# Segment sums on the vector engine, scan products held behind the next block's first product, and memory V products two steps sooner

## The chip, the cores and the metric

The kernel runs on one core of one Trainium2 chip. The metric is device time in microseconds (us) of one execution. The engines are named as the profile names them: PE is TensorE (PEld its weight loads), DVE is VectorE, ACT is ScalarE, POOL is GpSimd, SP is SyncE.

## The reference, cut to what matters

Two independent halves are computed and put side by side into a (1, 2048, 2048) bf16 result.

```python
# half A: a diagonal complex state space over 2048 steps, 1024 states
Bu = einsum('bld,pd->blp', x, B_bar)
for t in range(L):
    h = Lam_bar * h + Bu[:, t]
y = 2 * einsum('blp,dp->bld', hs, C).real + x * Dskip

# half B: 64 segments of 32 rows, 32 heads of 128, 8 memory rows carried from segment to segment
for s in range(64):
    h = concat([mem, x[s * 32:(s + 1) * 32]])      # 40 rows
    q, k, v = h @ Wq, h @ Wk, h @ Wv
    o = softmax(mask(q k^T / sqrt(128))) @ v @ Wo
    mem = o[:8]; out[s] = o[8:]
```

In half A the kernel rotates the complex recurrence into real scans: a block of 512 steps and 128 states is multiplied by a table of cosines and sines, scanned with a real decay, and multiplied back. In half B it does not run 64 segments one after the other: it takes a guess at the memory rows from the mean of each segment, works on all segments at once, and checks the guess at the end. The segment means of x are the "segment sums" of the title. The check and the fallback behind it are the same in all kernels here.

## The kernel before: what the change and the argument touch

There are 32 scan blocks (8 groups of states `pc`, 4 stretches of time `tb`). TensorE's instructions are pinned in program order. Each scan block is followed by four tiles of V products (`v_x`), so TensorE does 16 products into psU, then 32 into psP, and so on, for some 310 us. The other engines' order is chosen by a scheduler that follows the program, except where it says `keep_in_program_order`.

```python
def stage1(self, pc, tb):                          # one scan block
    t3, r3 = self.tabs
    u = k.ps("U", (128, 2, TB))                    # psU: two buffers
    for i in range(2):
        for c in range(KC):
            PE.matmul(u[:, i, :], self.bt[:, i, c, :], self.xT[:, c, ...], ...)          # 16 products
    pr = self.wp.tile([128, 2, 2, TB], FP32, name="a_pr", bufs=2)
    V.tensor_tensor(pr[:], u[:]..., view(t3, ...), ALU.mult)        # the first product: it frees psU
    w = pr[:, :, 0, :]
    V.tensor_tensor(w, w, pr[:, :, 1, :], ALU.add)
    g = self.wp.tile([128, 2, TB], BF16, name="a_g", bufs=2)
    for j in range(2):
        V.tensor_tensor_scan(w[:, j, :], rb, w[:, j, :], ...)
        S.activation(g[:, j, :], w[:, j, :], ACT.Copy)              # a_g, on ScalarE
    # ... carry into the next block, on GpSimd ...
    n = self.wp.tile([128, 2, 2, TB], BF16, name="a_n", bufs=1)
    h = self.wp.tile([128, 2, TB], BF16, name="a_h", bufs=2)
    V.tensor_tensor(n[:], g[:]..., view(r3, ...), ALU.mult)         # waits for a_g
    V.tensor_tensor(h[:], n[:, :, 0, :], n[:, :, 1, :], ALU.add)
    k.SP.dma_start(self.hs[tb][:, pc, :, :], h[:])

def v_x(self, hb, q, w):                           # four tiles of V
    st = self.next_st()                            # staging tile: two buffers
    for i in range(4):
        p = k.ps("P")[:]                           # psP: three buffers
        self.v_mm(p, w, 4 * q + i)                 # 8 products
        k.copy("s", st[:, i, :, 0:E], p...)        # the eviction psP -> b_vst, on ScalarE
    k.nc.scalar.dma_start(vx[...], st[...])        # the staging store b_vst -> b_vx, from ScalarE's queue

def sum_x(self, tmp):                              # segment sums of x, on TensorE
    # loads tile t of x (128 rows, row-major) as xr, four tiles ahead
    p = k.ps("R")
    for t in range(TT):                            # 16 tiles, one yield each
        for c in range(KC):
            k.PE.matmul(p[:, o:o + 4], xr[:, c * 128:(c + 1) * 128], k.ind[:], ...)      # 8 products of 4 columns
        yield
    # ... scaled into xbar ...

# main loop, for scan block n:
if n == 1: next(sx)
if n >= 3:
    for _ in range(2): next(sx, None)
a.stage1(pc, q)
if q == 2 and pc + 1 < PC:
    a.tables(pc + 1)                               # cosines, sines: VectorE and ScalarE

# second stage, step i of 32:
if i in (26, 28): vm = b.v_mem((i - 26) // 2, wv[(i - 26) // 2])     # V of the memory rows, heads 0-3 and 4-7
if 26 <= i < 30: next(vm)
```

## Time and profile before

| | before |
|---|---|
| median of 3 runs (lowest to highest) | 1243.47 us (1243.41 to 1243.81) |
| span of the profiled run, granted clock | 1241.5 us, 1.00 |
| scan stage, first psU product to first product of the second stage | 36.41 to 348.17 us |
| TensorE waits inside the scan stage | none |

The page's table of engines (busy time, share of the span, number of instructions), and the engine line of its chain of waits, which goes back from the last instruction to whatever released each step:

```profile
PE 1230.8 (99%) x8246; PEld 658.8 (53%) x8318; DVE 667.8 (54%) x1254; ACT 266.6 (21%) x695; POOL 278.1 (22%) x442
...
PE 96%; DMA 3%; issue 0%; SPq 0%; DVE 0%
```

TensorE is busy for all but about 11 us, and it is nearly the whole chain. So only two things can shorten the run: fewer TensorE instructions, or fewer TensorE waits. The waits of TensorE in the kernel before (who waits, for whom, us in total, times, longest):

```profile
PE psR L68 <- DVE hpb L109: 1.3, 1, 1.3
PE psO L68 <- DMA b_v<-b_vx: 0.9, 1, 0.9
PE psP L68 <- DMA b_wv<-in_B_Wv_dram: 0.4, 1, 0.4
PE psU L68 <- DMA b_xr<-in_B_x_dram: 0.3, 1, 0.3
```

Three of them belong to the start. The psO wait is the first attention product, which waits for V to be read back from memory; the timeline of TensorE shows it (start, us, instruction, tile, shapes, count, and in brackets the idle time just before with its releaser):

```profile
492.37 0.34 PE L68 MATMUL psS<-b_q,b_k 128*128 128x99 bf16 x4
493.59 0.50 PE L68 MATMUL psO<-b_v,b_m 128*128 128x129 bf16 x6 [0.88 <-DMA b_v<-b_vx]
```

TensorE's timeline in the scan stage shows one period: a psU block, the V tiles, then the segment sums' products, then the next block.

```profile
57.13 3.62 PE L68 MATMUL psU<-a_xT,a_bt 128*128 128x512 bf16 x16
60.58 7.07 PE L68 MATMUL psP<-b_wv,b_xe 128*128 128x512 bf16 x31
67.49 0.54 PE L68 MATMUL psR<-ind,b_xr 128*128 128x4 bf16 x16
67.89 3.61 PE L68 MATMUL psU<-a_xT,a_bt 128*128 128x512 bf16 x16
```

The block starts are 67.89 - 57.13 = 10.76 us apart. The 48 products of a block without sums take 48 x 215.8 ns = 10.36 us, so the sixteen small products cost 0.40 us of TensorE each time, eight times: 3.2 us. (The record counts 31 products where there are 32; single matmul records can be missing, and their ends are modelled, so starts are compared here, not ends.)

VectorE's groups between 30 and 345 us (line, engine, instruction, tiles, shapes, count; busy us, mean ns of one; idle us just before them with what ended it), and two reductions from the end of the program that serve as a price list:

```profile
L275 DVE TENSOR_TENSOR a_pr<-psU,a_tabf 128x2048 f32<-128x2048 f32 x32 | 73.0, 2282 | 16.2 <-PE psU L68 14.5 <-remote 1.6
...
L294 DVE TENSOR_TENSOR a_n<-a_g,a_tabh 128x2048 bf16<-128x2048 bf16 x32 | 39.1, 1223 | 16.8 <-ACT a_g L284 16.7
```
```profile
L887 DVE TENSOR_REDUCE c_ok<-c_a 128x1 f32<-128x704 f32 x1 | 0.9, 875 | 0.0
L887 DVE TENSOR_REDUCE c_ok<-c_a 128x1 f32<-128x208 f32 x1 | 0.4, 361 | 0.0
```

VectorE waits 16.7 us for `a_g`, the ScalarE copy that stands between its own scan and its own next product. That is the wait which the hold is meant to remove. How full each engine is, in stretches of 30 us (stretch, its length, busy us and count of PE, PEld, DVE, ACT, POOL, then the granted clock, the DMA share and GB/s):

```profile
60.00:90.00 30.00, 29.79 (x179) 14.21 (x182) 24.61 (x22) 13.60 (x24) 4.68 (x9) 1.00 0.72 196
90.00:120.00 30.00, 29.84 (x180) 14.24 (x182) 25.05 (x21) 11.73 (x21) 6.21 (x12) 1.00 0.50 140
120.00:150.00 30.00, 29.84 (x166) 14.06 (x168) 26.89 (x28) 11.31 (x20) 9.97 (x15) 1.00 0.54 162
```

VectorE is the second engine here, at 25 to 27 of 30 us. Anything moved onto it in this stretch takes it close to full.

### The profile page before, as it was taken

How to read it: one execution, taken by the hardware profiler on the slowest of the kernel's cores; microseconds unless marked ns; L12 is line 12 of the kernel's file. 1: busy time of each engine (PE TensorE's matmuls, PEld its weight loads, DVE VectorE, ACT ScalarE, POOL GpSimd, SP SyncE). 2: the span in 40 equal slices, each digit the busy share in tenths (PEclk: the TensorE clock that was granted, in tenths of full speed). 3: DMA queues.
4: the chain of work that ended last, by engine and by line, in shares of the span. 5: the costliest groups of instructions: out<-in, count | busy, mean ns of one | idle time of the engine just before them, and what ended most of it. 6: DMA issues, size and time to landing. Idle time of an engine off the chain costs nothing.

```text
span 1241.5 us, 20294 instructions
## 1 busy us (share of the span) xinstructions
PE 1230.8 (99%) x8246; PEld 658.8 (53%) x8318; DVE 667.8 (54%) x1254; ACT 266.6 (21%) x695; POOL 278.1 (22%) x442
## 2 busy tenths in 40 slices
PE   9999999999999999999999999999999999999998
PEld 4444444444455555556565656556565654445444
DVE  4688899998811124666666666666666641001000
ACT  5344344443310000111112121212111210000000
POOL 4111331222322330232223232222322220000000
PEclk9999999999999999999999999999999999999999
DMA  9965444644898834675464554545564279507000
GB/s 251 267 184 158 131 120 133 156 143 118 221 325 247 267 109 106 150 200 139 109 153 108 126 135 114 131 94 140 112 146 101 59 198 252 113 17 154 17 17 27
DMA packets 322357, 178.42 MB, mean 144 GB/s; under 512 B 144666, under 2 KB 307660, under 8 KB 322260
## 3 DMA queue, kind: packets, MB, share of 16 engines
q1 hardware_dynamic: 300164, 149.53, 49.4%
q10 hardware_dynamic: 21072, 24.38, 6.0%
q0 software_dynamic: 1024, 3.17, 0.7%
q8 instruction: 66, 1.08, 0.4%
q14 instruction: 31, 0.25, 0.1%
HBM read 89.14 MB, written 53.96 MB: 115 GB/s over the span
## 4 chain that ended last, share of the span: by engine, by line
PE 96%; DMA 3%; issue 0%; SPq 0%; DVE 0%
PE psP L68 80%; PE psU L68 9%; PE psS L68 3%; PE psO L68 2%; DMA b_v<-b_vx 2%; PE psR L68 2%; DMA b_wv<-in_B_Wv_dram 1%; SPq L68 0%; DVE b_ost L95 0%; DVE b_vm L572 0%
## 5 line engine op out<-in xcount | busy, mean ns | idle before, releaser
L68 PE MATMUL psP<-b_xe,b_wq 128*128 128x480 bf16 (+1 forms) x1280 | 247.5, 343 | 0.1
L68 PE MATMUL psP<-b_xe,b_wk 128*128 128x480 bf16 (+1 forms) x1280 | 247.5, 343 | 0.0
L68 PE MATMUL psP<-b_wv,b_xe 128*128 128x512 bf16 (+2 forms) x1033 | 223.5, 372 | 1.2 <-DMA b_wv<-in_B_Wv_dram 0.4
L694 POOL TENSOR_TENSOR b_m<-b_e,maskB 99x396 bf16<-99x396 bf16 (+1 forms) x160 | 134.4, 840 | 337.0 <-ACT b_e L693 337.0
L693 ACT ACTIVATE b_e<-psS 99x396 bf16<-99x396 f32 (+3 forms) x208 | 91.3, 441 | 531.7 <-PE psS L68 523.4
L68 PEld LDWEIGHTS <-b_wk 128*128 128x128 bf16 x1280 | 119.2, 98 | 94.2
L68 PEld LDWEIGHTS <-b_xe 128*128 128x128 bf16 x1056 | 101.8, 98 | 119.6 <-issue 0.7
L68 PEld LDWEIGHTS <-b_wq 128*128 128x128 bf16 x1280 | 118.5, 98 | 87.7
L95 DVE CAST b_k<-psP 128x480 bf16<-128x480 f32 (+1 forms) x192 | 97.3, 528 | 100.9 <-PE psP L68 100.9
L95 DVE CAST b_q<-psP 128x480 bf16<-128x480 f32 (+1 forms) x192 | 97.3, 528 | 92.2 <-PE psP L68 90.9
L68 PEld LDWEIGHTS <-b_ol 128*128 128x128 bf16 x864 | 84.3, 98 | 94.4
L68 PE MATMUL psU<-a_xT,a_bt 128*128 128x512 bf16 x493 | 113.9, 379 | 1.1
L68 PE MATMUL psP<-t,a_hl 128*128 128x512 bf16 x496 | 112.1, 379 | 0.8
L95 DVE CAST b_ost<-psP 128x512 bf16<-128x512 f32 (+1 forms) x17 | 11.5, 676 | 177.6 <-PE psP L68 176.6
L68 PE MATMUL psP<-wo,b_ol 128*128 128x512 bf16 (+1 forms) x440 | 91.9, 364 | 0.4
L68 PE MATMUL psP<-t,b_ol 128*128 128x512 bf16 x408 | 91.7, 379 | 0.4
L288 POOL TENSOR_SCALAR a_tt<-a_pr,a_tabf 128x1 f32<-128x1 f32 x48 | 34.0, 709 | 242.6 <-DVE a_pr L283 242.6
L93 ACT ACTIVATE b_vst<-psP 128x512 bf16<-128x512 f32 x126 | 72.0, 588 | 72.4 <-PE psP L68 65.1
L711 DVE TENSOR_TENSOR b_ob<-psO,b_accR 99x384 bf16<-99x384 f32 x160 | 86.0, 554 | 2.2
L275 DVE TENSOR_TENSOR a_pr<-psU,a_tabf 128x2048 f32<-128x2048 f32 x32 | 73.0, 2282 | 16.2 <-PE psU L68 14.5
L68 PEld LDWEIGHTS <-a_bt 128*128 128x128 bf16 x512 | 49.2, 98 | 57.6
L68 PEld LDWEIGHTS <-a_hl 128*128 128x128 bf16 x512 | 49.0, 98 | 56.7
(204 smaller groups left out, 969.7 us busy)
## 6 DMA issues: line engine op xcount, KB each, us to landing
b_v<-b_vx SPq DMA_DIRECT2D x16, 1122.0 KB
b_wv<-in_B_Wv_dram SPq DMA_DIRECT2D x16, 1024.0 KB
b_vx<-b_vst ACTq DMA_DIRECT2D x24, 544.0 KB
b_on<-b_ob SPq DMA_DIRECT2D x15, 720.0 KB
a_hs<-a_h SPq DMA_DIRECT2D x32, 256.0 KB
b_wog<-in_B_Wo_dram SPq DMA_DIRECT2D x4, 2048.0 KB
b_wq<-in_B_Wq_dram SPq DMA_DIRECT2D x16, 512.0 KB
b_wk<-in_B_Wk_dram SPq DMA_DIRECT2D x16, 512.0 KB
```

Of the source, the lines that this page charges most:

```text
L68: r = f(*a, **kw)
L93: self.S.activation(out, in_, ACT.Copy)
L95: self.V.tensor_copy(out, in_)
L275: V.tensor_tensor(pr[:], u[:].unsqueeze(1).to_broadcast([128, 2, 2, TB]), view(t3, [[TB + 1, 2], [TB + 1, 2], [1, TB]]), ALU.mult)
L288: G.tensor_scalar(tt[:, j:j + 1], w[:, j, TB - 1:TB], t3[:, 1, TB:TB + 1], None, ALU.mult)
L693: k.S.activation(e[:, a:b, :, 0:n], s[0:GW, a:b, :, 0:n], ACT.Exp, scale=float(E) ** -0.5, accum_out=self.accE[0:GW, j:j + 1])
L694: k.G.tensor_tensor(mv[:, a:b, :, 0:n], e[:, a:b, :, 0:n], mask[0:GW, :, 0:n].unsqueeze(2).to_broadcast([GW, b - a, 2, n]), ALU.mult)
L711: V.tensor_tensor(self.ob[:, b0:b0 + n, :], o[0:GW, 0:n, 0:E], r.unsqueeze(2).to_broadcast([GW, n, E]), ALU.mult)
```

## The change

The intent is to take the small products off TensorE and give the sums to VectorE, which has x already in the transposed tile `b_xe`; to make room there by holding the last two products of a scan block (`a_n`, `a_h`) until the first product of the next block is done, so that VectorE no longer waits for `a_g` and frees psU sooner; and to start the memory V products two steps sooner, so that V lands before the first attention product. The diff, with cuts marked:

```diff
 # consts: the tile ind and its five GpSimd fills are removed          (cut)

 def stage1(self, pc, tb):
+        self.form, last = None, self.form
         ...
         V.tensor_tensor(pr[:], u[:]..., ALU.mult)
+        if last is not None:
+            last()
         w = pr[:, :, 0, :]
         ...
-        n = ...; h = ...
-        V.tensor_tensor(n[:], g[:]..., ALU.mult)
-        V.tensor_tensor(h[:], n[:, :, 0, :], n[:, :, 1, :], ALU.add)
-        k.SP.dma_start(self.hs[tb][:, pc, :, :], h[:])
+        def form():
+            n = ...; h = ...
+            k.tc.keep_in_program_order(V.tensor_tensor(n[:], g[:]..., ALU.mult))
+            V.tensor_tensor(h[:], n[:, :, 0, :], n[:, :, 1, :], ALU.add)
+            k.SP.dma_start(self.hs[tb][:, pc, :, :], h[:])
+        self.form = form

 def sum_x(self, tmp):
-        # loads of x row-major, and 8 products psR<-ind,b_xr for each of 16 tiles       (cut)
+        xs = tmp.tile([128, KC, NSEG], FP32, name="b_xr", bufs=4)
+        for j in range(TT):
+            r = V.tensor_reduce(xs[:, :, 4 * j:4 * j + 4],
+                    self.xe[:, :, 128 * j:128 * j + 128].rearrange("p c (s t) -> p c s t", s=4), AX.X, ALU.add)
+            k.tc.keep_in_program_order(r)
             yield
         # ... scaled into xbar                                                           (cut)

 # v_mem, heads 8 and up: one transposing load instead of four
-            for h in range(4):
-                k.SP.dma_start_transpose(s[:, h, 0:E], self.vmt[hb][:, h * 128:(h + 1) * 128])
+            k.SP.dma_start_transpose(s[:, :, 0:E], self.vmt[hb][:])

 # main loop
-                if n == 1:
-                    next(sx)
-                if n >= 3:
-                    for _ in range(2):
-                        next(sx, None)
                 a.stage1(pc, q)
+                for _ in range(2):
+                    next(sx, None)
 ...
+            a.form()                       # behind the last block

 # second stage
-                if i in (26, 28):
-                    vm = b.v_mem((i - 26) // 2, wv[(i - 26) // 2])
-                if 26 <= i < 30:
+                if i in (24, 26):
+                    vm = b.v_mem((i - 24) // 2, wv[(i - 24) // 2])
+                if 24 <= i < 28:
                     next(vm)
```

More of the change, by code (lines that the diff above doesn't have):

```diff
@@ L110, in consts @@
     k.S.activation(k.hpe[:], k.hpb[:], ACT.Exp)
-    k.ind = c.tile([128, 4], BF16, name="ind")
-    G.memset(k.ind[:], 0.0)
-    for j in range(4):
-        G.memset(k.ind[32 * j:32 * j + 32, j:j + 1], 1.0)
 def masks(k):
@@ L167, in __init__ @@
         self.Cre, self.Cim, self.logdt, self.Dskip, self.out = Cre, Cim, logdt, Dskip, out
+        self.form = None
         self.hs = [k.drp.tile([128, PC, 2, TB], BF16, name=f"a_hs{i}") for i in range(NB)]
@@ L291, in stage1 @@
             self.carry = nx
-        n = self.wp.tile([128, 2, 2, TB], BF16, name="a_n", bufs=1)
-        h = self.wp.tile([128, 2, TB], BF16, name="a_h", bufs=2)
-        V.tensor_tensor(n[:], g[:].unsqueeze(1).to_broadcast([128, 2, 2, TB]), view(r3, [[TB, 2], [TB, 2], [1, TB]]), ALU.mult)
-        V.tensor_tensor(h[:], n[:, :, 0, :], n[:, :, 1, :], ALU.add)
-        k.SP.dma_start(self.hs[tb][:, pc, :, :], h[:])
+        def form():
+            n = self.wp.tile([128, 2, 2, TB], BF16, name="a_n", bufs=1)
+            h = self.wp.tile([128, 2, TB], BF16, name="a_h", bufs=2)
+            k.tc.keep_in_program_order(
+                V.tensor_tensor(n[:], g[:].unsqueeze(1).to_broadcast([128, 2, 2, TB]), view(r3, [[TB, 2], [TB, 2], [1, TB]]), ALU.mult))
+            V.tensor_tensor(h[:], n[:, :, 0, :], n[:, :, 1, :], ALU.add)
+            k.SP.dma_start(self.hs[tb][:, pc, :, :], h[:])
+        self.form = form
     def s2_tiles(self, hpool, pool):
@@ L424, in sum_x @@
     def sum_x(self, tmp):
-        k = self.k
-        xrs = {}
-        def load(t):
-            if t < TT:
-                xrs[t] = tmp.tile([128, D], BF16, name="b_xr", bufs=4)
-                k.SP.dma_start(xrs[t][:], self.x[0][t * 128:(t + 1) * 128, :])
-        for t in range(4):
-            load(t)
-        yield
-        p = k.ps("R")
-        for t in range(TT):
-            xr = xrs.pop(t)
-            for c in range(KC):
-                o = c * NSEG + 4 * t
-                k.PE.matmul(p[:, o:o + 4], xr[:, c * 128:(c + 1) * 128], k.ind[:], start=True, stop=True)
-            load(t + 4)
+        k = self.k; V = k.V
+        xs = tmp.tile([128, KC, NSEG], FP32, name="b_xr", bufs=4)
+        for j in range(TT):
+            r = V.tensor_reduce(xs[:, :, 4 * j:4 * j + 4], self.xe[:, :, 128 * j:128 * j + 128].rearrange("p c (s t) -> p c s t", s=4),
+                                AX.X, ALU.add)
+            k.tc.keep_in_program_order(r)
             yield
-        pv = p[:].rearrange("p (c s) -> p c s", c=KC)
+        e = NSEG - 4
         ms = tmp.tile([128, KC], FP32, name="b_ms", bufs=1)
-        k.V.tensor_reduce(ms[:], self.m0T[:], AX.X, ALU.add)
-        k.V.tensor_scalar(self.xbar[:], pv, 1.0 / L, None, ALU.mult)
-        k.V.tensor_tensor(ms[:], ms[:], pv[:, :, 0], ALU.add)
-        k.V.tensor_scalar(self.xbar[:, :, 0], ms[:], 1.0 / L, None, ALU.mult)
+        V.tensor_reduce(ms[:], self.m0T[:], AX.X, ALU.add)
+        V.tensor_tensor(xs[:, :, e], xs[:, :, e], ms[:], ALU.add)
+        V.tensor_scalar(self.xbar[:, :, 2:NSEG - 2], xs[:, :, 0:e], 1.0 / L, None, ALU.mult)
+        V.tensor_scalar(self.xbar[:, :, 0:2], xs[:, :, e:e + 2], 1.0 / L, None, ALU.mult)
+        V.tensor_scalar(self.xbar[:, :, NSEG - 2:NSEG], xs[:, :, e + 2:NSEG], 1.0 / L, None, ALU.mult)
         yield
```

## The prediction

It was written before the changed kernel ran.

> **Bound.** TensorE: the engine table has PE busy 1230.8 of 1241.5 us, and the chain of waits is 96% PE. The stretch table gives 29.84 of every 30 us in most of the scan stage (30 to 330 us) and 500.0 of 500 us in attention. PE idles about 10 us: start, tail, and one wait between: 0.88 us at 493.6 us, where the first attention product waits for the first V tile (25.9 us from issue to landing in the chain). Only TensorE work or waits that go away move the time.
>
> **What changes.**
> 1. 128 four-column products (psR<-ind,b_xr) go. Scan blocks come 10.36 us apart without them, 10.76 us with sixteen, eight times: -3.2 us, all critical. Some 4 MB of loads go too; PE did not wait for them. The rest of PE's order is the same, but for the memory V products, which stand 6.9 us earlier.
> 2. So the V loads start about 6.9 us sooner: -0.9 us. One transposing load for four costs PE nothing.
> 3. VectorE gets 16 reductions of 1024 elements, two behind each of the first eight blocks. The trace has reductions of 208 and 704 elements at 361 and 875 ns: about 1.2 us each by estimate, 19 us. The Trainium skill ("VectorE: DVE Perf Modes", perf-mode tier table) gives a reduce only the 1x mode, in bf16 too; 205 ns for 64 bf16 elements agree.
> 4. a_n and a_h go behind the next block's first product. VectorE's wait of 0.70 us for a_g goes (24 times, 16.7 us in the table of waits), and independent work comes between dependent steps: about 0.5 us a block.
>
> **On the critical path.** Items 3 and 4 only through lateness. Before, VectorE starts on a block at most 3.7 us after its products end, and a psU pair is free 5.5 us or more before TensorE needs it. After, a block costs about 7.6 us and 2.3 us of reductions in a period of 10.4 us, and 3 us of tables every fourth block; after blocks 6 and 7, back to back, VectorE should be 6 to 9 us late (my tally with durations of the trace; for before it gives the lateness within 0.3 us in most blocks). psU still holds, but ScalarE's queue is in order: it now evicts three psP tiles, waits for both scans (a_g), then evicts the fourth. TensorE, with three psP banks, then stalls 0.5 to 1.5 us near blocks 7 to 10 (105 to 135 us), and once near the stage's end: 0 to 3.5 us in all, by estimate 1.9. So most of item 1 may be paid back.
>
> Sum: 1243.5 - 3.2 - 0.9 + 1.9 = 1241.3 us; eight times in ten between 1238.9 and 1243.6. Chances: faster by over 2% 0.01, within 2% 0.98, slower 0.01.
>
> **What would show it.** Ind products gone, blocks 10.36 us apart from 2 to 6; no VectorE wait for a_g; a reduce of about 1.2 us; no TensorE wait at the first V product. If the stalls come: psP products idle 0.5 us or more, put down to ScalarE, between 105 and 140 us, with VectorE full from 80 to 150 us. If not: 29.8 of 30 us there, and about 1239.4 us.
>
> **What would make it wrong.** A slower reduce (one strided reduction of 1120 elements took 2155 ns, not 1.3 us): each 0.1 us adds nearly 1 us of stall. A cheaper VectorE block: no stalls. Sooner V loads may collide with others.

## The result, and the profile after

| | before | after |
|---|---|---|
| median of 4 runs (lowest to highest) | 1243.44 us (1243.30 to 1243.81) | 1242.10 us (1242.03 to 1242.23) |
| ratio, 95% interval | | 0.9989 [0.9972, 1.0006] |
| span of the profiled run | 1241.5 us | 1240.5 us |
| first psU product / first product of the second stage | 36.41 / 348.17 us | 36.69 / 348.15 us |

Ratios are the mean time of one kernel's fast runs over the mean of the other's of the same rounds, so not quite the ratio of the medians quoted. The changed kernel is 1.3 us faster by the medians, which is the same within 2%. The predicted 1241.3 us is 0.8 us too low, and the result lies inside the range.

The table of engines and the chain's engine line, after:

```profile
PE 1227.9 (99%) x8120; PEld 655.4 (53%) x8190; DVE 676.9 (55%) x1271; ACT 268.1 (22%) x695; POOL 268.3 (22%) x437
...
PE 92%; DVE 4%; DMA 2%; issue 1%; ACT 0%; SPq 0%; another core or an unknown queue 0%; ACTq 0%; DVEq 0%
```

VectorE has appeared in the chain with 4%: at some points TensorE now waits, through ScalarE as will be seen, for VectorE's work. TensorE's period, and two of VectorE's groups between 30 and 345 us, after:

```profile
57.41 3.62 PE L68 MATMUL psU<-a_xT,a_bt 128*128 128x512 bf16 x16
60.86 7.07 PE L68 MATMUL psP<-b_wv,b_xe 128*128 128x512 bf16 x31
67.77 3.62 PE L68 MATMUL psU<-a_xT,a_bt 128*128 128x512 bf16 x16
```
```profile
L297 DVE TENSOR_TENSOR a_n<-a_g,a_tabh 128x2048 bf16<-128x2048 bf16 x31 | 37.7, 1216 | 0.0
...
L433 DVE TENSOR_REDUCE b_xr<-b_xe 128x32 f32<-128x1024 bf16 x16 | 18.6, 1202 | 0.0
```

The period is 67.77 - 57.41 = 10.36 us, the wait for `a_g` went from 16.7 us to nothing, and a reduction takes 1202 ns. The first attention product no longer waits:

```profile
492.35 0.34 PE L68 MATMUL psS<-b_q,b_k 128*128 128x99 bf16 x4
492.53 0.50 PE L68 MATMUL psO<-b_v,b_m 128*128 128x129 bf16 x6
```

The waits of TensorE after (its two other waits of the start, 1.3 and 0.4 us, are as before and left out), and the stretches:

```profile
PE psP L68 <- ACT b_vst L93: 2.3, 4, 0.9
PE psU L68 <- DMA b_xr<-in_B_x_dram: 0.8, 1, 0.8
```
```profile
60.00:90.00 30.00, 29.84 (x138) 13.62 (x140) 28.23 (x24) 13.03 (x23) 3.87 (x9) 1.00 0.50 156
90.00:120.00 30.00, 29.84 (x138) 13.58 (x139) 29.93 (x29) 10.11 (x18) 4.46 (x12) 1.00 0.31 96
120.00:150.00 30.00, 28.72 (x132) 12.93 (x133) 29.93 (x32) 13.21 (x24) 8.57 (x14) 1.00 0.42 121
```

A new wait has come, four times, for ScalarE's eviction of a psP tile, while VectorE is full for 60 us. The clock stays at 1.00. TensorE's and ScalarE's timelines show the first and largest of the four:

```profile
116.11 5.34 PE L68 MATMUL psP<-b_wv,b_xe 128*128 128x512 bf16 x23
122.40 1.89 PE L68 MATMUL psP<-b_wv,b_xe 128*128 128x512 bf16 x8 [0.94 <-ACT b_vst L93]
```
```profile
120.05 0.63 ACT L284 ACTIVATE a_g<-a_pr 128x512 bf16<-128x512 f32 x1 [2.24 <-DVE a_pr L283]
120.59 0.71 ACT L238 ACTIVATE a_k<-a_tabf,a_bim 128x512 f32<-128x512 f32 x1
121.23 0.63 ACT L284 ACTIVATE a_g<-a_pr 128x512 bf16<-128x512 f32 x1
121.77 0.58 ACT L93 ACTIVATE b_vst<-psP 128x512 bf16<-128x512 f32 x1
```

These `a_g` copies belong to block 7 (counted from 0). Its products are the second half of this line of TensorE, and its first product on VectorE is the line below:

```profile
98.85 7.07 PE L68 MATMUL psU<-a_xT,a_bt 128*128 128x512 bf16 x32
```
```profile
113.67 2.28 DVE L273 TENSOR_TENSOR a_pr<-psU,a_tabf 128x2048 f32<-128x2048 f32 x1
```

Read TensorE's and ScalarE's timelines from below. The fourth psP tile of the four that began at 116.11 needs the bank of the first. The first tile's eviction started at 121.77, behind the two `a_g` copies of block 7 in ScalarE's order; ScalarE stood idle for 2.24 us ahead of them, waiting for VectorE's scan. VectorE had started on block 7 at 113.67, 7.75 us after its products ended (98.85 + 7.07 = 105.92), while before the change its largest lateness was 3.72 us. ScalarE itself had time to spare. The Trainium skill ("Perfetto Trace Analysis", Matmuls) says that independent groups of products should rotate through the PSUM banks, so that evacuation of one overlaps the next. The kernel does that with three banks, and the trace agrees with the advice as far as it goes: the rotation hides a late eviction until the eviction is later than the three banks' 24 products.

The other waits are 0.24 us at 133.15, of the same kind, and two at the end of the scan stage:

```profile
337.99 7.07 PE L68 MATMUL psP<-b_wv,b_xe 128*128 128x512 bf16 x31 [0.65 <-ACT b_vst L93]
345.50 1.89 PE L68 MATMUL psP<-b_wv,b_xe 128*128 128x512 bf16 x8 [0.44 <-ACT b_vst L93]
```

**The account of the two profiled runs.** The scan stage took 311.76 us before and 311.46 us after: 0.30 us less, where 3.2 us of products had gone. So the waits cost 2.9 us, though the idle times add up to 2.27 us. The difference is in how an idle time is reckoned: 24 products from 116.11 at 215.8 ns each would let the next start at 121.29, it started at 122.40, and the loss is 1.11 us where the record says 0.94 idle. The modelled end of a matmul hides about 0.16 us at each wait. Beyond the stage, the V wait gives 1.06 us (0.88 us idle and the same hidden 0.18 us), and the start of the stage lies 0.28 us later. That last figure need not be due to the change: run 11 apart, the stage starts anywhere between 36.34 and 37.05 us, with waits of 0.2 to 1.2 us in all for the first loads ahead of it.

### The profile page after: what moved, and what is told of

It is laid out like the page before. It is cut to its first block, busy times and chain, and to the rows that moved or that the text cites. A ratio compares the mean times of both kernels' runs of the same rounds, so it can differ in the third digit from the quotient of the medians.

```text
span 1240.5 us, 20010 instructions
## 1 busy us (share of the span) xinstructions
PE 1227.9 (99%) x8120; PEld 655.4 (53%) x8190; DVE 676.9 (55%) x1271; ACT 268.1 (22%) x695; POOL 268.3 (22%) x437
## 3 DMA queue, kind: packets, MB, share of 16 engines
q0 software_dynamic: 1024, 3.17, 0.7%
q8 instruction: 65, 1.06, 0.4%
## 4 chain that ended last, share of the span: by engine, by line
PE 92%; DVE 4%; DMA 2%; issue 1%; ACT 0%; SPq 0%; another core or an unknown queue 0%; ACTq 0%; DVEq 0%
PE psP L68 78%; PE psU L68 7%; PE psS L68 3%; PE psO L68 2%; PE psR L68 1%; DMA b_vx<-b_vst 1%; DVE a_pr L283 1%; DVE a_pr L273 1%; DVE b_xr L433 1%; DVE a_pr L278 1%; DMA b_wv<-in_B_Wv_dram 1%; ACT b_vst L93 0%; SPq L68 0%; DVE a_h L298 0%
```

## The experiments

The theory: the products are worth 3.2 us and the V wait 1.1 us; two chains eat into that. VectorE's lateness reaches TensorE through ScalarE's ordered queue (122 and 133 us), and the hold of the last block delays evictions at the stage's end (338 and 345 us). The rivals are named with each run. Each ran five timed rounds. Runs 1 to 4, runs 5 to 8 and runs 9 to 11 each share a chip and the runs of the kernel before.

| run | median | before, same rounds | ratio [95%] |
|---|---|---|---|
| 1 V products sooner, alone | 1242.28 | 1243.39 | 0.9990 [0.9976, 1.0004] |
| 2 hold, alone | 1251.24 | 1243.39 | 1.0064 [1.0050, 1.0077] |
| 3 sums on VectorE, alone | 1247.22 | 1243.39 | 1.0029 [1.0016, 1.0043] |
| 4 changed kernel, sums earlier | 1240.62 | 1243.39 | 0.9977 [0.9963, 0.9990] |
| 5 hold alone, products of the sums moved | 1244.81 | 1243.46 | 1.0012 [0.9998, 1.0025] |
| 6 run 4, last block's products not held behind | 1240.97 | 1243.46 | 0.9984 [0.9970, 0.9997] |
| 7 kernel before, each small product twice | 1246.63 | 1243.46 | 1.0025 [1.0012, 1.0039] |
| 8 changed kernel, fills kept | 1242.07 | 1243.46 | 0.9990 [0.9977, 1.0004] |
| 9 run 6, 1 MB of loads later | 1239.22 | 1243.32 | 0.9967 [0.9953, 0.9980] |
| 10 run 4, the same loads later | 1239.72 | 1243.32 | 0.9971 [0.9958, 0.9985] |
| 11 changed kernel, copies of a_g behind the evictions | 1249.39 | 1243.32 | 1.0047 [1.0033, 1.0060] |

### 1. The memory V products sooner, alone

```diff
 # in the kernel before
-                if i in (26, 28):
-                    vm = b.v_mem((i - 26) // 2, wv[(i - 26) // 2])
-                if 26 <= i < 30:
+                if i in (24, 26):
+                    vm = b.v_mem((i - 24) // 2, wv[(i - 24) // 2])
+                if 24 <= i < 28:
```

> The kernel before with only the first memory Vs two steps sooner. Theory (late load of the first V tile): the 0.88 us TensorE wait at about 493 us goes, nothing else moves, so 0.9 us faster: about 1242.6 us. Rival (the wait was hidden elsewhere, or the earlier loads collide with others and bring a new wait): within 0.3 us of before, 1243.2 to 1243.8 us.

It took 1.11 us off the median, and TensorE's timeline has no wait at the first attention product (it starts at 492.71 us, directly behind the scores). The part is worth the wait that it removes, and the loads it moves collide with nothing that shows.

### 2. The hold, alone

```diff
 # in the kernel before: form() in stage1, called behind the next block's first product, and at the end
+        self.form, last = None, self.form
 ...
+        if last is not None:
+            last()
 ...
-        n = ...; h = ...; (products and store)
+        def form(): ...
```

> The kernel before with only the a_n and a_h products held behind the next block's first product; the 128 four-column products stay. Theory A (the hold alone costs at the end of the scan stage, the reductions alone in its middle): no TensorE wait for ScalarE at 100 to 140 us, but 0.9 to 1.1 us of such waits in the last 15 us of the scan stage, so about 1244.4 us. Rival B (all TensorE waits of the changed kernel come from the reductions): no wait anywhere, 1243.4 us. Rival C (the hold is a gain by itself, since VectorE waits 16.7 us less): below 1243 us.

This missed by 7 us: it is 7.85 us slower than the kernel before. The two waits at the stage's end came as theory A had them (0.65 us at 345.99, 0.31 us at 353.36), but TensorE's timeline shows one large wait more, near the start of the stage:

```profile
49.94 3.03 PE L68 MATMUL psP<-b_wv,b_xe 128*128 128x512 bf16 x8 [4.43 <-ACT b_vst L93]
52.77 4.20 PE L68 MATMUL psU<-a_xT,a_bt 128*128 128x512 bf16 x16
```

ScalarE's timeline shows why the eviction was late; the first line is the issue of the fourth staging store (the expectation of run 5 calls it the third):

```profile
48.29 0.43 ACTq L513 DMA_DIRECT2D b_vx<-b_vst  x1
48.77 0.63 ACT L238 ACTIVATE a_k<-a_fr 128x513 f32<-128x513 f32 x1 [11.26 <-DMA b_xe<-in_B_x_dram]
```

The queue stood for 11.26 us. It did not wait for a DMA that it needs: the store reads the staging tile, which ScalarE had just written. The profile puts the wait down to a transposing load of x, ended at 48.22 us. In the built programs the store waits, besides ScalarE's own work, on one of eight DMA completion semaphores, shared out among the transfers in order: semaphore 2 in this kernel, whose user before was a load into `b_xe`; semaphore 6 in the kernel before and in the changed one, whose user before was a load into `a_xT`. There the queue stood for 2.27 and 3.25 us at this store. So the order of unrelated transfers decides what this store waits for, and the hold changed that order.

The idle time also cooled the clock. The stretch from 50 to 55 us (columns as above; the granted clock is the third figure from the end):

```profile
50.00:55.00 5.00, 5.00 (x16) 1.89 (x16) 0.00 (x0) 2.49 (x5) 0.00 (x0) 0.66 1.19 315
```

Eight products took 3.03 us instead of 1.89, and the next sixteen 4.20 instead of 3.62: 1.7 us more on top of the wait. The Trainium skill ("TensorE: Matmul & The Clock Gate", What's actually happening) states that an idle window of about 3.4 us drops TensorE to half its clock and that about 3.4 us of work bring it back. The trace agrees: 3.4 of 5 us at half the clock make a mean of 0.66, an estimate from that page's figure, and 0.66 is what is recorded; waits of 1.62 us and less left the clock at 1.00 (in run 11 the eight products after the wait of 1.62 us took 1.89 us).

### 3. The sums on VectorE, alone

```diff
 # the changed kernel without the hold, V products at their old place
-        if last is not None:
-            last()
-        def form(): ...
+        n = ...; h = ...; (products and store at the end of stage1, as before)
-                if i in (24, 26):
+                if i in (26, 28):
```

> The kernel before with only the segment sums on VectorE, two reductions behind each of the first eight blocks' first instructions as the scheduler places them; products not held, memory Vs at the old place. Theory A (VectorE's lateness passes through ScalarE's in-order queue to TensorE): VectorE is later than in the changed kernel, TensorE waits of about 6 us for psP evictions in 90 to 200 us, minus 3.2 us of products: about 1246.5 us (range 1244 to 1248). Rival (lateness of VectorE does not reach TensorE; the waits in the changed kernel have another cause, such as the staging writes): 3.2 us less, 1240.3 us.

It is 3.83 us slower than the kernel before, as expected: the 3.2 us of products were gained and about 7 us lost. The largest wait in TensorE's timeline stands one step of V tiles ahead of the changed kernel's first one, and is four times as long; in the profiled run it cooled the clock too (a mean of 0.66 from 115 to 120 us; the mean clock of the five rounds goes from 0.997 to 1.000, so the drop may not come in each):

```profile
114.69 2.81 PE L68 MATMUL psP<-b_wv,b_xe 128*128 128x512 bf16 x8 [3.76 <-ACT b_vst L93]
```

Two smaller waits follow, 0.68 us at 208.14 and 0.83 us at 350.06. So the hold earns its place only beside the sums. Sums alone and V sooner would come to about 1247.2 - 1.1 = 1246.1 us, an estimate from runs 1 and 3; the whole change, with the hold, takes 1242.1 us. The hold is worth about 4 us there.

### 4. The changed kernel with the reductions spread earlier

```diff
             sx = b.sum_x(p1)
+            for _ in range(4):
+                next(sx)
 ...
                 a.stage1(pc, q)
-                for _ in range(2):
+                for _ in range(3 if n < 3 else 1):
                     next(sx, None)
```

The same 16 reductions, but four ahead of the first block, three behind each of the next three, and then one a block. Nothing else is changed, so this tells VectorE's lateness from any other cause of the waits at 122 and 133 us.

> The changed kernel with its 16 reductions spread otherwise: four ahead of the first block, three behind each of the first three blocks, then one a block; same work, same holds. Theory A: VectorE is at most some 5 us late, so the TensorE waits of 0.94 us at 122 us and 0.24 us at 133 us go, those at 338 and 345 us (0.65 and 0.44 us) stay: about 1.2 us faster than the changed kernel, 1240.9 us. Rival (ScalarE's staging writes of the V tiles hold up the evictions): all four waits stay, 1242.1 us.

It gained 1.4 us on the changed kernel (2.77 us under its own runs of the kernel before, where the changed kernel is 1.34 us under its own). VectorE is at most 4.0 us late, and the waits at 122 and 133 us are gone, while those at the end stay:

```profile
336.14 7.07 PE L68 MATMUL psP<-b_wv,b_xe 128*128 128x512 bf16 x32 [0.65 <-ACT b_vst L93]
343.98 1.89 PE L68 MATMUL psP<-b_wv,b_xe 128*128 128x512 bf16 x8 [0.77 <-ACT b_vst L93]
```

The cause of the first two waits is shown: not the amount of VectorE's new work, but two reductions a block in a stretch that had room for less than that.

### 5. The hold alone again, with the products of the sums behind the block

```diff
 # in run 2
-                if n == 1: next(sx)
-                if n >= 3: (two steps of sx)
                 a.stage1(pc, q)
+                if n == 1: next(sx)
+                if n >= 3: (two steps of sx)
```

This moves the sums' loads to where the changed kernel has its sums, and with them the sharing of semaphores. One theory of run 2 is the shared semaphore; its rival is that the hold itself delays ScalarE near 48 us.

> The hold alone again, but with the loads and products of the segment sums after the block's products instead of ahead of them. The aim is to move one thing: which earlier transfer the third staging store on ScalarE's queue has to wait for (the completion semaphore it shares: in the run before it was that of a load that ended at 48.2 us, here that of one that ends near 40 us). Theory (the 4.4 us TensorE wait at 45 to 50 us of the hold-only run, and the slow clock behind it, come from that shared semaphore): the wait is gone, TensorE waits at the end of the scan stage of 0.6 to 1.1 us remain, 1244.0 to 1244.6 us. Rival (the hold itself delays the evictions there): still 1251 us.

The 4.43 us wait is gone (the store waits for the load into `a_xT` again, on semaphore 6 as in the kernel before, and the queue stands for 2.09 us), and the kernel is 1.35 us slower than before, 0.2 us above the range expected. What is left are two waits, 0.65 us at 339.72 and 0.33 us at 347.12: the same pair that the changed kernel has at its end. With the hidden part of each they make about 1.3 us, the cost of the hold here; runs 6 and 10 tell which of the two is the hold's own work. The large miss of run 2 was not. The edit also moves the products, so it is a strong hint and not proof of the semaphore.

### 6. Run 4, with the last block's products not held behind their successor

```diff
 # on run 4
-        if last is not None:
+        end = pc == PC - 1 and tb == NB - 1
+        if last is not None and not end:
             last()
 ...
+        if end:
+            last()                  # behind the scans of the last block
```

> The early reductions, and in the very last block the held products come after its scans instead of between its first product and its addition. Theory (the 0.65 us TensorE wait near 336 us is the hold's: the held products put the last block's scans 1.8 us later, and the second wait near 344 us is a staging store issued late for the same reason): both waits go or fall under 0.3 us, about 1.1 us faster than the early reductions alone, 1239.5 us. Rival (they come from the traffic of the next stage's loads, whatever the order on VectorE): the waits stay, 1240.6 us.

This missed. The 0.65 us wait went, as expected of the hold delaying the last block's scans and so the evictions behind them. But the second wait grew from 0.77 to 1.56 us, and the median did not fall (1240.97, with rounds from 1240.56 to 1243.00). Two lines of ScalarE's timeline, with others between them:

```profile
334.33 0.37 ACTq L503 DMA_DIRECT2D b_vx<-b_vst  x1
344.02 1.57 ACT L93 ACTIVATE b_vst<-psP 128x512 bf16<-128x512 f32 x3 [5.46 <-DMA b_vx<-b_vst]
```

The last evictions write into a staging tile whose store, issued at 334.33 us, has not landed before 344.02 us. In run 4 the same evictions were let go at 343.33 us, in a run whose stage began 0.7 us sooner. So the store, not the evictions before it, sets this moment, and removing one wait lengthened the next. The DMA engines are 99% and 95% busy from 335 to 345 us: from 329.83 to 336.4 us GpSimd's queue issues four loads of `a_hl` (512 KB each), the broadcast of Dskip and three loads of x (256 KB each), all for the second stage.

### 7. Each small product twice

```diff
 # in the kernel before
+                for _ in range(2):
                     k.PE.matmul(p[:, o:o + 4], xr[:, c * 128:(c + 1) * 128], k.ind[:], start=True, stop=True)
```

> The kernel before with each of the 128 four-column products done twice, which gives the same result. Theory (they cost TensorE 0.40 us for sixteen): 3.2 us slower, 1246.6 us. Rival (part of them hides in TensorE's waits, or they hold up loads): under 2 us slower.

The second set of 128 products cost 3.17 us. The term of 3.2 us in the prediction is measured by itself.

### 8. The changed kernel with the fills kept

```diff
+    k.ind = c.tile([128, 4], BF16, name="ind")
+    G.memset(k.ind[:], 0.0)
+    for j in range(4):
+        G.memset(k.ind[32 * j:32 * j + 32, j:j + 1], 1.0)
```

This asks whether the five GpSimd fills that the change removes explain the stage's start, 0.28 us later.

> The changed kernel with the five small fills on GpSimd kept at the start that the change removes. The changed kernel's first block of the scan starts at 36.69 us, against 36.41 us before, and its second transposing product waits 0.80 us for an x load, against 0.28 us. Theory (without the fills GpSimd's transfers start sooner and delay that load): 0.2 to 0.4 us faster than the changed kernel, 1241.8 us. Rival (that load's landing just varies between executions): no difference, 1242.1 us, and other runs show starts on both sides.

1242.07 us, the same as the changed kernel. The start simply varies.

### 9. Run 6, with 1 MB of second-stage loads behind the staging stores

```diff
 # on run 6, s2_tiles and load_xn
+        q = self.k.nc.scalar
-        q.dma_start(self.dB[:], ...)
+        self.k.tc.keep_in_program_order(q.dma_start(self.dB[:], ...))
 ...
-        q.dma_start(self.xns[t][:], ...)
+        self.k.tc.keep_in_program_order(q.dma_start(self.xns[t][:], ...))
```

The Dskip broadcast and the three loads of x go from GpSimd's queue, where they ran at 332 us and on, to ScalarE's, behind the last staging store.

> Early reductions and the last block's held products after its scans, and in addition the 1 MB of loads for the next stage's skip term (b_x row copies and their factor; not needed before 351 us) issued on ScalarE's queue behind the last staging store instead of on GpSimd's at 331 to 335 us. Theory (the 1.56 us TensorE wait near 344 us is for a staging buffer whose store shares the DMA engines, 95 to 99% busy from 335 to 345 us, with those loads): the wait falls to under 0.6 us, about 1 us faster than without, 1239.7 us. Rival (the 2 MB of a_hl loads alone fill the engines, or the buffer waits for something else): the wait stays at 1.2 us or more, 1240.9 us.

1239.22 us is the best time: 4.1 us under the kernel before, and about 2.8 us under the changed kernel (each against its own runs of before). TensorE has no wait at all for an eviction in the scan blocks; ScalarE still waits for the store, but 2.27 us instead of 5.46:

```profile
323.38 20.88 PE L68 MATMUL psP<-b_wv,b_xe 128*128 128x512 bf16 x94
```
```profile
340.26 1.19 ACT L93 ACTIVATE b_vst<-psP 128x512 bf16<-128x512 f32 x2 [2.27 <-DMA b_vx<-b_vst]
```

The store and the loads come from different queues, and yet the loads delayed it. That agrees with the Trainium skill ("Trainium Kernel Development and Optimization", Key Constraints), which says that DMAs from SP, ACT and POOL run on the same 16 engines and interleave: with that 1 MB out of the way the evictions that wait for the store of 0.5 MB were let go at 340.26 us instead of 344.02 (run 6). From the store's own issue this is 6.5 us against 9.7, but run 10 below, with the same loads moved, has 9.4 (331.09 to 340.49). A steadier measure is the time from the issue of the first `a_hl` load, whenever the store itself was issued: 14.2 us in runs 4 and 6, 13.9 in the changed kernel and 13.1 in the kernel before, against about 11 in runs 9 and 10.

### 10. Run 4, with the same loads later

> Early reductions and the late loads of the skip term, the held products of the last block as in the changed kernel. Theory: the wait of 0.65 us near 336 us stays (it is the hold's), the one of 0.77 us near 344 us goes (it is the traffic's): 1239.9 us, 0.7 us faster than the early reductions alone. Rival (both belong together): no gain, 1240.6 us.

The edit is that of run 9 without that of run 6. It took 1239.72 us; the wait at 336 us stays at 0.65 us and the second is gone. So of the two waits at the end, the first belongs to the hold and the second to the store. Run 3, which has no hold, agrees: it has none of the first kind, and its wait of 0.83 us at 350.06 is of the second (ScalarE was let go by a store at 349.41). Each can be removed by itself, and run 9 has neither.

### 11. The changed kernel, with the copies of a_g pinned behind the evictions

```diff
 # on the changed kernel
         for j in range(2):
             V.tensor_tensor_scan(w[:, j, :], ...)
-            S.activation(g[:, j, :], w[:, j, :], ACT.Copy)
 ...
         def form():
+            for j in range(2):
+                k.tc.keep_in_program_order(S.activation(g[:, j, :], w[:, j, :], ACT.Copy))
 # evictions on ScalarE are kept in program order too
```

If it is only the order of ScalarE's queue that carries VectorE's lateness into TensorE, then putting the evictions of a block ahead of its `a_g` copies should move the wait to where that order meets it.

> The changed kernel, with its reductions where they were, but on ScalarE both a_g copies of a block are pinned behind all four evictions of the V step that follows, and so, where two blocks stand together, ahead of the first eviction of the next step. VectorE's work and order stay. Theory (what TensorE waits for is an eviction that stands behind an a_g copy in ScalarE's in-order queue): the waits near 122 and 133 us go, and one of 1.5 to 2.5 us comes at about 109 to 112 us, where four a_g copies now stand ahead of four evictions; small ones may come after the other pairs of blocks; total 1242 to 1243.5 us. Rival (TensorE waits because VectorE is late in freeing psU, or for the staging stores): the waits stay at 122 and 133 us.

The part about the middle came as expected: no wait at 122 or 133 us, and one a block sooner:

```profile
119.19 1.89 PE L68 MATMUL psP<-b_wv,b_xe 128*128 128x512 bf16 x8 [1.62 <-ACT b_vst L93]
```

This kernel's stage starts 6.47 us later than the changed kernel's, so 119.19 here is 112.7 on the other's clock, against 109 to 112 us expected. Small ones came after other pairs of blocks as well (0.23 us at 210.37, 0.35 us at 302.32), and one of 0.95 us at 353.00 near the stage's end. The total missed by 6 us: the pin also fixed ScalarE's order in the first 30 us, where an eviction then stood behind table work. TensorE waited 3.89 us at 25.13 us and ran at a mean clock of 0.50 in the five microseconds after it, and about 6.5 us were lost there. That start was not tested by itself.

## Why the prediction was right, point by point

- **The bound.** Right. TensorE is the chain, and each microsecond gained or lost in the runs is a TensorE instruction or a TensorE wait.
- **The small products, 3.2 us.** Right. The blocks are 10.36 us apart (57.41, 67.77, 78.13, 88.49, 98.85), and doubling the products costs 3.17 us.
- **The V wait, 0.9 us.** Right and slightly small: 1.06 us in the trace, 1.11 us in run 1, because the idle figure leaves out some 0.18 us.
- **The reduction, 1.2 us.** Right: 1202 ns. The Trainium skill ("VectorE: DVE Perf Modes", the perf-mode tier table) gives a reduction no fast mode, in bf16 either, and 2x to a bf16 product. The trace agrees: 1024 bf16 elements take 1202 ns as a reduction and 685 ns as an addition of two tiles (`a_h`), while 1024 f32 elements take 1219 ns as an addition.
- **The hold.** Right in what it does to VectorE: the 16.7 us of waits for `a_g` are gone. A block with two reductions takes 113.67 - 104.00 = 9.67 us of VectorE, of which 2.23 us are the reductions; the prediction had 7.6 and 2.3.
- **The lateness, 6 to 9 us.** Right: 7.75 us at block 7 and 7.07 us at block 8, with VectorE at 29.93 of 30 us from 90 to 150 us.
- **The waits, 1.9 us.** The mechanism was right (ScalarE's order, three psP banks, between 105 and 140 us, and at the end), and the size was short: they cost 2.9 us. This is the term of the sum that was mis-sized. About 0.6 us of it is the hidden part of four waits, which the prediction left out. The rest is at the stage's end, where "once" was twice: run 10 shows that the second wait has a cause of its own, the staging store among the second stage's loads, which the prediction did not see. One detail of the mechanism differs too: the prediction had the `a_g` copies ahead of a step's fourth eviction, and so they stand while VectorE keeps up (at 67.45 us, say), but at the waits of 122, 133 and 338 us they stand ahead of the first.
- **"So most of item 1 may be paid back."** Right: 2.9 of 3.2 us.

With the mended term the sum is 1243.5 - 3.2 - 1.1 + 2.9 = 1242.1 us, which is the measured median. The agreement to the last digit is luck: the start of the stage alone varies by 0.7 us. Nor is the sum an independent test, since the 2.9 us were themselves read from the lengths of the stage in the two profiled runs.

What stays open: the single transposing load for heads 8 and up was not run by itself; the part of the semaphore in run 2 is seen in the program and the trace, and was not isolated; and in run 11 the loss at the start was only read from the profile.

## What to carry to other kernels

When work is moved from the bounding engine to one that is nearly as full, follow the second engine's lateness through every ordered queue that serves both: here VectorE never held TensorE up directly, but a ScalarE copy that waited for VectorE stood in front of the eviction that TensorE needed. Spread such work over the slack that is there (run 4 took the same reductions and lost 1.4 us less) before judging the move. When one wait is removed and the time stays, look for the next wait with a fixed end, such as a store that lands when the DMA engines let it (run 6), and remove that as well (run 9).

## What the Trainium skill lacked or had wrong

- No page that was read puts the order of ScalarE's queue and the rotation of PSUM banks together and says that an eviction can stand behind a copy that waits for another engine. "Perfetto Trace Analysis" (Matmuls) gives the rotation alone; here three banks in rotation did not help once VectorE was 7.75 us late (0.94 us of TensorE idle at 122.40), and spreading the reductions did.
- No page that was read gives the cost in time of completion semaphores shared among unrelated DMAs: run 2's ScalarE queue stood for 11.26 us before a store, put down to an unrelated load, TensorE waited 4.43 us, and in run 5 that wait was gone.
- "TensorE: Matmul & The Clock Gate" (Back-to-back issue gap) gives about 131 ns as the sustained spacing of products of 512 columns in a real kernel and calls the 216 ns formula one for isolated products. Here the sustained spacing is 215.8 ns (48 products in 10.36 us, with weight loads and the clock at 1.00); the formula held here and the sustained figure did not.
